# K and Q of later tiles projected with tokens stationary and laid out by transposing DMAs

## The chip, the cores and the metric

The kernel runs on one core of a Trainium2 chip. A core has a matrix engine (TensorE, PE, with its weight loads shown as PEld), VectorE (DVE), ScalarE (ACT), GpSimd (POOL), and SyncE (SP), which here only issues DMAs. Each engine works through its own queue in order and waits for others by semaphores; sixteen DMA engines move the data. The metric is the device time of one execution in microseconds, given as the median of several runs.

## The reference

A block of a transformer with two halves, on 2048 tokens of width 448, in bf16. Six modulation vectors come from a conditioning row. The first half is attention with 16 heads of width 28, in which each query sees itself and the 255 tokens before it. The second is a gated MLP whose gate is mixed over the tokens by a full 2048 x 2048 matrix.

```python
mod = (_silu(c) @ w_mod).reshape(c.shape[0], 6, 1, -1)
sa, ca, ga, sb, cb, gb = ...
h = _layernorm(x, axis=-1) * (1 + ca) + sa
x = x + ga * _A_ref(h, A_wqkv, A_wo)
h = _layernorm(x, axis=-1) * (1 + cb) + sb
x = x + gb * _B_ref(h, B_w_in, B_w_sp, B_b_sp, B_w_out)
# _A_ref: q, k, v = x @ wqkv; softmax over the window of 256; (p @ v) @ wo
# _B_ref
z = _gelu(jnp.einsum('bsd,df->bsf', x, w_in))
z1 = z[..., :Fh].copy()
z2 = _layernorm(z[..., Fh:], axis=-1)
g = jnp.einsum('ts,bsf->btf', w_sp, z2) + b_sp[None, :, None]
return jnp.einsum('bsf,fd->bsd', z1 * g, w_out)
```

## The kernel before

The tokens are 16 tiles of 128, in four blocks of four tiles. The work has three stages. In the first, attention, each tile is normalized (statistics on DVE, the reciprocal root on POOL), turned so that the width lies on the partitions (block 0 by PE, blocks 1 to 3 by transposing DMAs from `xn` into `hT`), modulated in place, and projected to Q, K and V. Scores, exponentials, masks, the product with V, the output projection and the second normalization follow per tile. In the second stage PE computes the two halves of the MLP's input (`z2` at L1120, `z1T` at L1141). In the third it multiplies with the spatial matrix (L1166) and the output matrix (L1185). The spatial matrix comes from memory through 32 transposing DMAs of 128 x 1024: 16 into `wspA`, which the first half of the third stage needs whole, and 16 into `wspB`.

Heads are 28 wide, and the scores are computed with 32 rows per head, four heads beside each other on PE's rows. So Q and K must stand as 4 groups of 4 heads x 32 rows (28 used), tokens along the free axis. `WQK` holds the weights padded to 32 columns per head. For K, one tile at a time: 4 groups x 4 chunks of the width, 16 matmuls with 128 weights columns stationary and 128 tokens streamed (L821), copied to `KT` by ACT or DVE (L833, L834). For Q of blocks 1 to 3, a whole block at a time: 4 groups x 4 chunks of 512 tokens (L763), copied to `qT` (L772, L773). Some of the queries' far halves are also needed in a block-diagonal form, `QBD`, in which each head's queries stand on that head's rows only: four copies of 32 rows per block make it (L790, L791), and one pair of matmuls per tile uses it (L967). V is projected with the tokens stationary and 448 columns of unpadded weights streamed (L841).

The order of all work is fixed ahead. Each operation has a number; the string `PLAN` lists them, a letter for the engine (p, a, d, t, s for PE, ACT, DVE, POOL and SP), the number, and the buffers it takes. Each engine runs its part of the list in order, and semaphore waits are derived from the data and the buffers. The list is the result of a search, with durations and waits of a model. `turn` is the helper that issues a transposing DMA on SP: turned are the normalized rows (`xn`, `xn2`), the attention output (`o_sb`) and the spatial matrix. SP runs these and the plain loads and stores in one queue.

Of the kernel before, what the change touches and what calls it, by code (L numbers as in the profile page):

```python
# [5 lines left out]
BF16 = mybir.dt.bfloat16  # L6
# [6 lines left out]
a0 t30 d24 s1 d27 d26 d25 d23 d22 p51.1 t31 p60.3 s2 t32 p52.2 t35 p59.0 s4 p61.1 p55.0 s6 a3 p58.0 p63.0 a5  # L13
s10 t36 p40.1 a7 s8 p69.2 a9 p75.3 d114 s12 p65.1 p53.0 t33 d112 p68.2 s11 t34 p54.3 d115 p77.0 d113 p50.3 s13
a41 p71.0 t116 a43 p46.0 s15 d117.0 t29 p74.2 d118.3 p62.0 p64.2 p47 a42 a44 p57.0 p48.1 d106 d86 p76.0 p49
a107 t104 p129.6 p67.3 d87 d105 p126.4 t37 a130 p82.3 p56.3 t111 p84.1 d127 p81.1 p73.1 a131 p83.3 p66.0 d128
t38 p72.0 p141.1 d110 d121 p78.0 a108 t109 p70.2 p150.3 d119 p142 d122 d120 p79.2 d184 p151 t123 a143 p138.0
a152 t28 d125.2 p139 d124.3 p85.0 p147.6 d178 a140 p132.2 d185 p148 d182 a133 p144.7 d179 d180 p135.1 a134
p153.0 d183 a136 d181 p371.0 d246 t186 a137 p145 d248 p154 a372.4 t39 p165.1 d187.3 t190 d242 s194 p166 t188
a149 t192 d45 p377.0 a146 d373 p156.6 d167 a378.6 t189.1 p157 d244 p159.7 t191.2 a158 p395.0 d193.0 a155 s196  # L20
d379 p172.6 a396.5 d249 d247 p173 d243 p175.1 a174 s197 p160 d88 t89 d245 a397 p176 d168 p94.0 t250 p95 d177
s195 a171 p402.0 a161 d96 t254 p97.1 t256 a403.1 p98 d398 s14 d375 p162.7 d400 p374.0 p163 a404 d381 p90.0 d99
p376 d201 a199 p422.0 d198 d251.0 p380 p382 d200 p91 s258 a423.0.0 p211.1 d93 d92 d407 d170 d252 p212 p218.0
d255.1 t253.2 a164 d383 s260 p429.0 d169 a213 t257.3 p219 a430.3 p399.1 p205.1 s16 d220 p206 d384.2 p202.0
d306 s385 p203 a207 d426 p401 p447.0 a204 p208.1 s804 a448.4.1 d310 p209 d405 p227.0 d431 p228 s259 t102
p424.1 p406 p408 a425 p454.0 d229 a210 d409 p427.0 d312 a455.1 p230.0 t101 d410.1 p221.1 p231 d216 d214 d451
s411 t103 p428 p222 a232 p80.3 p472.0 d456 s261 a223 p432 a215 p224.0 a473.5.2 p225 s21 p233.1 p433 s807
p449.0 d434 t100 d226 a217 p479.0 d435.0 a450 t262 p234 d308 s436 a480.0 p474.0 p236.0 t263 d311 d313 d235
p452.0 p237 d476 s806 p453 a475 p496.0 a238 d307 d481 t265 d264 p412.1 a497.3.0 p457 p386.0 p387 p458 d309
d459 d388 d460.1 t314 t320 p413 p498.0 p521.0 a499 a522.1.1 p272.0 d414 p523.0 p273 p269.1 s461 p270 p477.0  # L30
d415 d274 d321.2 d316 s20 p503.0 a271 d500 t317.3 p275.0 p478 s323 p276 p266.1 p267 p482 a504.4 a524 p546.0
p483 t318 d389 d277 d319.1 a268 d505 d484 p282.0 d390 d278 p283 a547.5.2 p437.1 p548.0 p438 s18 d485.1 d525
p501.0 p528.0 d439 d440 d315.0 s486 s325 a284 a529.0 a549 a279 p502 p288.0 p291.1 p292 p289 d290 p553.0 d530
d293 p506 p507 p239.0 s322 p240 a554.3 a241 p526.1 t391 p527 s324 p531 a280 d550 p571.0 p532 p462.0 d508 d281
d416 d509.2 d392.1 d533 d441 t442 t417 a572.4.0 p463 p294.1 d534.1 d464 p573.1 p295 p578.0 a296 p300.0 s510
p285.1 p286 a579.0 p551.1 p301 p552 p595.0 d555 t329 t418 d327 d287 d302 d575 p511.1 p512 p556 d513 t328 a326
a596.1.1 a574 p336.0 p337 p557 p602.0 s535 p576.0 a338 p577 d558 d559.0 a603.3 p536.0 d393 p339.1 p537 p340
d580 p620.0 d538 d599 a341 p581 p297.0 p597.0 s17 s394 p487.1 d465 p298 a621.6.2 d539 a598 a299 p488 p582
p645.0 d583 p600.1 s808 d584.1 p622.1 p333.0 d489 p330.1 d624 d604 d466 p331 p334 a646.4.0 s585 d490 a332
p627.0 p601 t467 t443 t468 d335 d491 p346.1 d345 t444.1 p605 p347 p586.0 p587 a628.0 a348 p652.0 p358.1 d514  # L40
d649 a623 s560 a653.1 d588 p359 p606 p349.0 p350 p625.0 d629 a360 a351 p670.0 d589 d654 d607 p352.1 p303.0
p304 s19 a671.2.1 p353 p626 a344 a305 d608.2 t469.2 p630 p677.0 d354 d419.0 p631 p647.0 p364.1 a678.6 p561.0
p562 p365 d342 a648 p694.0 d420 t445 d674 d632 d343 d540 t470 s446 d633.0 p650.1 s803 a366 p672.1 d679 d563
a695.5.2 s609 d564 p367.1 p651 s421 t492 p655 p368 p656 p701.0 t541 a673 t542 d543.1 d657 p355.0 p675.0 a369
a702.3 t544 d658.2 p676 d493.0 p680 p356 d698 d565 d357 p696.0 p681 t566 d515 d682 p719.0 a697 d494 d590
# [1223 lines left out]
```

## Time and profile before

| what | value |
|---|---|
| time, three runs | 275.18 to 275.75 us, median 275.42 us |
| the profiled execution | span 273.2 us from the first to the last instruction |
| busy in the span | PE 267.1, PEld 155.3, DVE 160.4, ACT 126.4, POOL 111.4 us |
| attention, 20 to 107.6 us | PE 86.0, ACT 81.1, DVE 80.8 us busy |
| MLP input, 107.6 to 152.7 us | PE 45.0, DVE 37.3, ACT 27.9 us busy |
| spatial and output matrix, 152.7 to 270.6 us | PE 117.4 us busy |
| granted TensorE clock | 1.00 throughout |

The profile shows one execution. Its span leaves out what lies around the instructions, which the runs' times take in. PE's busy time is not its peak, because matmuls are pipelined; a length in the chain of waits (start, length, what) is the nearest to what an instruction costs in a row of others. The chain follows the work that ended last backwards, from each step to what released it. A group's row gives line, engine, operation, output and inputs, shapes and count, then the busy time, the mean of one in ns, and the idle time before it with what ended it.

### The profile page before, as it was taken

The numbers are of one execution on the slowest core, as the hardware profiler recorded it, in microseconds if no ns is written. First come the engines' busy times: TensorE is split into PE (matmuls) and PEld (weight loads), VectorE is DVE, ScalarE is ACT, GpSimd is POOL, SyncE is SP. The second block draws the span as 40 slices with busy tenths as digits, with TensorE's granted clock in tenths as the row PEclk, the third lists the DMA queues.
The fourth block names the chain that finished last, engine by engine and source line by source line (L and its number), as shares of the span: only waits on it lengthen the run. The fifth ranks groups of instructions, "written<-read, shape, count | busy, mean of one in ns | idle before, by whom it ended". The sixth has DMA issues, their size and how long they took to land.

```text
span 273.2 us, 8371 instructions
## 1 busy us (share of the span) xinstructions
PE 267.1 (98%) x3741; PEld 155.3 (57%) x3751; DVE 160.4 (59%) x344; ACT 126.4 (46%) x149; POOL 111.4 (41%) x147
## 2 busy tenths in 40 slices
PE   8999999999999999999999999999999999999996
PEld 6976676777667866554554444444444444444453
DVE  3798999989889999949889210221222022152244
ACT  5799999899989988567666400000000000000000
POOL 6455298305033286547448003354543023061330
PEclk9999999999999999999999999999999999999999
DMA  7999846453234573957789996000000000001003
GB/s 209 299 244 132 127 103 122 122 101 109 64 103 67 91 73 72 185 117 134 117 176 175 217 186 118 0 0 0 2 0 0 0 2 0 34 17 36 34 34 118
DMA packets 67301, 25.54 MB, mean 93 GB/s; under 512 B 58497, under 2 KB 66178, under 8 KB 67266
## 3 DMA queue, kind: packets, MB, share of 16 engines
q1 hardware_dynamic: 66016, 24.02, 44.5%
q10 hardware_dynamic: 1250, 0.99, 1.3%
q8 instruction: 29, 0.48, 0.7%
q14 instruction: 6, 0.05, 0.1%
HBM read 9.01 MB, written 1.84 MB: 40 GB/s over the span
## 4 chain that ended last, share of the span: by engine, by line
PE 80%; ACT 8%; DMA 6%; DVE 3%; SPq 2%; issue 1%
PE ps L1166 35%; PE ps L1120 8%; PE ps L1141 8%; PE ps L1185 8%; ACT PW L912 6%; DMA wmodB<-in_w_mod_dram 6%; PE ps L1000 5%; PE ps L956 4%; PE ps L1026 4%; PE ps L763 3%; PE ps L821 2%; PE ps L841 2%; DVE PT L973 1%; ACT QBD L790 1%; PE ps L967 1%
## 5 line engine op out<-in xcount | busy, mean ns | idle before, releaser
L1173 POOL TENSOR_TENSOR z1T<-tmpg,z1T 128x512 bf16<-128x512 bf16 x28 | 32.0, 1152 | 77.3 <-DVE tmpg L1170 77.3
L912 ACT ACTIVATE PW<-ps 128x2048 bf16<-128x2048 f32 (+1 forms) x42 | 59.9, 1452 | 5.4 <-PE ps L956 3.9
L1170 DVE TENSOR_TENSOR tmpg<-ps,bsp_bc 128x512 bf16<-128x512 f32 x28 | 18.9, 689 | 73.8 <-PE ps L1166 62.6
L1166 PE MATMUL ps<-wspB,z 128*128 128x512 bf16 x219 | 49.7, 379 | 0.3
L1166 PE MATMUL ps<-wspA,z 128*128 128x512 bf16 x219 | 49.1, 379 | 0.4 <-issue 0.2
L633 POOL TENSOR_TENSOR rs_all<-mv_all,neghalf 128x1 f32<-128x1 f32 (+2 forms) x37 | 22.5, 635 | 45.6 <-DVE mv_all L631 45.6
L1166 PEld LDWEIGHTS ps<-wspA,z 128*128 128x128 bf16 x224 | 21.8, 98 | 26.6 <-issue 0.4
L1166 PEld LDWEIGHTS ps<-wspB,z 128*128 128x128 bf16 x224 | 21.9, 98 | 26.2
L973 DVE TENSOR_TENSOR PT<-PW,mask 128x2048 bf16<-128x2048 bf16 x28 | 34.0, 1219 | 0.0
L1000 PE MATMUL ps<-Vaug,PT 128*128 128x32 bf16 x496 | 25.8, 177 | 0.0
L1000 PEld LDWEIGHTS ps<-Vaug,PT 128*128 128x128 bf16 x496 | 22.9, 96 | 3.3 <-issue 0.4
L1120 PE MATMUL ps<-w_in,hT 64*128 64x448 bf16 x224 | 22.0, 349 | 0.0
L1185 PE MATMUL ps<-w_out_g,z1T 128*128 128x448 bf16 (+2 forms) x119 | 22.0, 341 | 0.0
L1141 PE MATMUL ps<-hT,w_in 64*128 64x512 bf16 x196 | 22.0, 376 | 0.0
L1000 PE MATMUL ps<-Vaug,PW 128*128 128x32 bf16 x224 | 21.2, 176 | 0.0
L629 DVE BATCH_NORM_STATS2 st_all<-z 128x6 f32<-128x448 bf16 x32 | 18.4, 608 | 4.4 <-ACT z L1127 4.3
L629 DVE BATCH_NORM_STATS2 st_all<-x_sb 128x6 f32<-128x448 bf16 x32 | 19.2, 614 | 2.7 <-DMA x_sb<-in_A_x_dram 2.5
L1195 DVE TENSOR_TENSOR fin<-ps,x_sb 128x448 bf16<-128x448 f32 (+1 forms) x16 | 9.5, 612 | 16.7 <-PE ps L1185 11.6
L1000 PEld LDWEIGHTS ps<-Vaug,PW 128*128 128x128 bf16 x224 | 17.9, 96 | 1.9
L821 PE MATMUL ps<-hT,WQK 112*128 112x128 bf16 x256 | 18.7, 219 | 0.0
L1149 ACT ACTIVATE z1T<-ps 128x512 bf16<-128x512 f32 x28 | 14.5, 603 | 8.8 <-PE ps L1141 8.7
L956 PE MATMUL ps<-qT,KT 32*128 32x128 bf16 (+5 forms) x1344 | 17.1, 197 | 0.9 <-ACT PW L912 0.6
(108 smaller groups left out, 355.0 us busy)
## 6 DMA issues: line engine op xcount, KB each, us to landing
wmodB<-in_w_mod_dram SPq DMA_DIRECT2D x1, 1568.0 KB, 15.3
out_dram<-fin SPq DMA_DIRECT2D x14, 112.0 KB, 1.7
x_sb<-in_A_x_dram SPq DMA_DIRECT2D x3, 448.0 KB, 7.9
w_in<-in_B_w_in_dram SPq DMA_DIRECT2D x3, 448.0 KB, 4.2
w_out_g<-in_B_w_out_dram SPq DMA_DIRECT2D x1, 784.0 KB, 6.4
bsp_bc<-in_B_b_sp_dram SPq DMA_DIRECT2D x1, 512.0 KB, 5.3
x_sb<-in_A_x_dram SPq DMA_DIRECT2D x2, 224.0 KB, 4.9
hT<-xn SPq DMA_TRANSPOSE x28, 2.9
```

The costliest lines, as they stand in the source:

```text
L629: st = [dve(0.62, lambda e, t=t, o=12 - 6 * (n - ci), s=s: e.bn_stats(st_all[:, slot, t, o:o + 6], s()), deps(t), prio) for ci, s in enume ...
L633: return pool(0.4 + 0.15 * len(tiles), lambda e: e.tensor_tensor(rs_all[:, slot, a:b], mv_all[:, slot, a:b, 1], neghalf[:, 0:b - a], ALU.pow),
L821: km = lambda g, kc, start, stop, h=h, t=t: lambda e: e.matmul(ps[:, h.slot[0], g * 128:(g + 1) * 128], lhsT=WQK[0:CP, kc, 16 + 4 * g:20 + ...
L912: ex = act(xdur, lambda e, out_ap=out_ap, in_ap=in_ap: e.activation(out_ap(), in_ap(), ACT.Exp, scale=SCALE), [s] + list(after), v - 8.0 + ...
L956: fm.append(lambda e, hm=hm, qi=qi, key=key, kn=kn, lo=lo, hi=hi, col=col, p0=p0, t=t, j=j: e.matmul(ps[p0:p0 + kn, hm.slot[t], col:col + ...
L973: mk2 = lock_d(1.2, lambda e, hp=hp, at_w=at_w, pad=pad, at_f=at_f, cols=cols, j=j: e.tensor_tensor(cols(hp.slot[0] * 2048, [[256, 8], [12 ...
L1000: fns.append(lambda e, hp=hp, hO=hO, hi=hi, bi=bi, kb=kb, hd=hd, nb=nb, a=at[hi][bi], p_of=p_of: e.matmul(ps[:, hO.slot[0], 32 * hd:32 * h ...
L1120: return lambda e, kc, p0, start, stop: e.matmul(ps[:, hs[t % 2].slot[hf], 0:D], lhsT=hT[p0:p0 + 64, kc, t * 128:(t + 1) * 128], rhs=w_in[ ...
L1141: return lambda e, kc, p0, start, stop: e.matmul(ps[:, hs[b // 2].slot[b % 2], :], lhsT=w_in[p0:p0 + 64, kc, ft * 128:(ft + 1) * 128], rhs ...
L1166: m = pe(16 * MMS, [lambda e, h=h, si=si, ft=ft, tb=tb: e.matmul(ps[:, h.slot[0], :], lhsT=z2[:, si, ft * 128:(ft + 1) * 128], rhs=(wspA i ...
L1173: u = pool(1.16, lambda e, ht=ht, ft=ft, tb=tb: e.tensor_tensor(z1T[tb][:, ft, :], tmpg[:, ht.slot[0], :], z1T[tb][:, ft, :], ALU.mult), [ ...
L1185: return [lambda e, ft=ft: e.matmul(ps[:, h.slot[0], 0:hi - lo], lhsT=z1T[t // 4][:, ft, (t % 4) * 128:(t % 4 + 1) * 128], rhs=w_out_g[:, ...
```

## The change

For tiles 4 to 15 Q and K are projected like V: the 128 tokens of a tile are stationary, and 448 columns of unpadded weights are streamed, four matmuls for K and four for Q (L805 in the changed kernel). ACT or DVE copies the result, tokens on the partitions, into a staging tile with the heads 32 columns apart: one copy for K into one of two `kst` (L817, L818), two copies for Q into one of two `qst` (L835, L836; even and odd groups apart). A transposing DMA on SP then lays each out: `kst`, 512 columns, into a ring of 8 tiles that is now `KT`, and `qst`, 1280 columns, into a ring of 4 tiles, `qring`. Of its ten blocks of 128 columns two are plain groups and eight hold one head each of the other groups with zeros around it, so that the block-diagonal form comes out of the same transfer. The zeros are set once (POOL, L531 and L532). The copies into `QBD` remain for block 0 alone, and tiles 0 to 3 are projected as before. `qring` and the staging tiles lie in the first half of `wspA`, so those eight loads wait until all scores and all turns of Q and K are done. The waits that paced the projections are gone. The list of the order was searched anew, so the order on all engines differs.

```diff
+    KR, QR, QB_N = 8, 4, 10
+    KT, kt_off, _ = alloc("KT", [128, 4, KR * 128], BF16)
+    wq_st, _, _ = alloc("wq_st", [128, DC, 2 * D], BF16)
+    kst = [alloc("kst0", [128, H, 32], BF16)[0]]
...
-    QBD, _, qbd_bytes = alloc("QBD", [128, 2, 4, 2, 256], BF16, at=wspA_off)
-    qT, _, qt_bytes = alloc("qT", [128, 2, 4, 512], BF16, at=wspA_off + qbd_bytes)
+    qring, _, qr_bytes = alloc("qring", [128, QR, QB_N, 128], BF16, at=wspA_off)
+    qst, _, qs_bytes = alloc("qst", [128, 2, QB_N * 128], BF16, at=wspA_off + qr_bytes)
+    kst.append(alloc("kst1", [128, H, 32], BF16, at=wspA_off + qr_bytes + qs_bytes)[0])
...
+    t_qsz = [pool(0.8, lambda e, i=i: e.memset(qst[:, i, :].bitcast(F32), 0.0), prio=-60.0) for i in range(2)]
+    t_ksz = [pool(0.2, lambda e, i=i: e.memset(kst[i][:, :, DH:32], 0.0), prio=-60.0) for i in range(2)]
...
-            mms = [lambda e, h=h, g=g, kc=kc, tb=tb: e.matmul(
-                ps[:, h.slot[0], :], lhsT=WQK[0:CP, kc, 4 * g:4 * g + 4, :].rearrange("p a b -> p (a b)"),
-                rhs=hT[0:CP, kc, tb * 512:(tb + 1) * 512], start=(kc == 0), stop=(kc == DC - 1)) for kc in range(DC)]
-            m = pe2(4 * MMS, mms, [evs, t_wqk], v + 1 + k * 0.1, [h])
...
+                def by_tokens(part, h, t=t, evs=evs, v=v):
+                    return pe2(4 * MMD, [lambda e, kc=kc: e.matmul(
+                        ps[:, h.slot[0], 0:D], lhsT=hT[0:CP, kc, t * 128:(t + 1) * 128], rhs=wq_st[0:CP, kc, part * D:(part + 1) * D],
+                        start=(kc == 0), stop=(kc == DC - 1)) for kc in range(DC)], [evs, (t_wk, t_wq)[1 - part]], v + 1, [h])
...
+                K_ready[t] = turn("d_k%d" % t, lambda t=t: KT[:, :, t % KR * 128:(t % KR + 1) * 128], lambda hs=hs: kst[hs.slot[0]][:].rearrange("p h e -> p (h e)"), [ev], v + 1)
+                hs.until.append(K_ready[t])
...
+                Q_ready[t] = turn("d_q%d" % t, lambda t=t: qring[:, t % QR], lambda hs=hs: qst[:, hs.slot[0], :], [q_evs], v + 1, lat=1.6)
+                hs.until.append(Q_ready[t])
...
-        deps = [t_mB, t_gg] if si > 7 else [S_of[8], S_of[9], S_of[10], S_of[11], S_of[WSP][0], q_dma[2]] if si in (0, 1, 4, 5) else [all_S, list(q_dma.values())]
+        deps = [t_mB, t_gg] if si > 7 else [all_S, [Q_ready[t] for t in range(4, NT)], [K_ready[t] for t in range(4, NT)]]
```

Three places of the order. SP late in attention, about tiles 10 to 15; before, it holds the turns of the attention output (`o_sb`) and of the second normalization (`xn_91`, the tile `xn2`) and a few loads:

```order
L432 DMA w_in<-in_B_w_in_dram 128x1792
L465 DMA_TRANSPOSE hT<-xn_91 128x4x128
L465 DMA_TRANSPOSE wspA<-in_B_w_sp_dram 128x1024
L465 DMA_TRANSPOSE hT<-o_sb 128x4x128
L465 DMA_TRANSPOSE hT<-xn_91 128x4x128
L465 DMA_TRANSPOSE hT<-o_sb 128x4x128
```

The same stretch of the changed kernel, where `xn_95` is `xn2` and `kst_76` and `kst_87` are the two staging tiles:

```order
L471 DMA_TRANSPOSE KT<-kst_76 128x4x128
L471 DMA_TRANSPOSE KT<-kst_87 128x4x128
L471 DMA_TRANSPOSE hT<-o_sb 128x4x128
L471 DMA_TRANSPOSE hT<-xn_95 128x4x128
L471 DMA_TRANSPOSE hT<-o_sb 128x4x128
L471 DMA_TRANSPOSE KT<-kst_76 128x4x128
L471 DMA_TRANSPOSE qring<-qst 128x10x128
```

The turns of K and Q stand between those that were there, and the early loads of `wspA` have left.

SP after attention, from the load of the output matrix on; before:

```order
L861 DMA w_out_g<-in_B_w_out_dram 128x7x448
L465 DMA_TRANSPOSE wspA<-in_B_w_sp_dram 128x1024 x2
L465 DMA_TRANSPOSE hT<-o_sb 128x4x128
L465 DMA_TRANSPOSE hT<-xn_91 128x4x128 x4
L465 DMA_TRANSPOSE wspB<-in_B_w_sp_dram 128x1024
L465 DMA_TRANSPOSE wspA<-in_B_w_sp_dram 128x1024 x2
L465 DMA_TRANSPOSE hT<-xn_91 128x4x128 x3
L465 DMA_TRANSPOSE wspA<-in_B_w_sp_dram 128x1024
L465 DMA_TRANSPOSE hT<-xn_91 128x4x128
L465 DMA_TRANSPOSE wspA<-in_B_w_sp_dram 128x1024 x5
L465 DMA_TRANSPOSE wspB<-in_B_w_sp_dram 128x1024
L465 DMA_TRANSPOSE wspA<-in_B_w_sp_dram 128x1024
```

In the changed kernel, from the turn of tile 15's normalized rows (the last of the two `xn_95` here) to the last load of `wspA`:

```order
L471 DMA_TRANSPOSE wspB<-in_B_w_sp_dram 128x1024
L471 DMA_TRANSPOSE hT<-xn_95 128x4x128 x2
L471 DMA_TRANSPOSE wspB<-in_B_w_sp_dram 128x1024 x2
L471 DMA_TRANSPOSE wspA<-in_B_w_sp_dram 128x1024 x3
L471 DMA_TRANSPOSE wspB<-in_B_w_sp_dram 128x1024
L471 DMA_TRANSPOSE wspA<-in_B_w_sp_dram 128x1024 x3
L471 DMA_TRANSPOSE wspB<-in_B_w_sp_dram 128x1024
L471 DMA_TRANSPOSE wspA<-in_B_w_sp_dram 128x1024
```

Between the last turn of `xn2` and the last load of `wspA` stood 6 large loads of `wspA` and one of `wspB`; now 7 and 4. Counted from the load of the output matrix there were 11 of `wspA`, 2 of `wspB` and 9 turns, and now there are 14, 6 and 9, behind a first load of `wspB` that waits for the last probabilities.

DVE around a copy of K late in attention; before, that of tile 14, from PSUM to `KT`:

```order
L1014 RECIPROCAL rec_all<-ps 128x16
L1016 TENSOR_TENSOR o_sb<-ps,rec_all 128x4x112
L834 CAST KT<-ps 128x4x128
L651 TENSOR_SCALAR xn_91<-x_sb,rs_all,nm_all 128x448
L791 COPY QBD<-qT 32x512
```

In the changed kernel that of tile 13, from PSUM to the staging tile:

```order
L1026 TENSOR_TENSOR o_sb<-ps,rec_all 128x4x112
L983 TENSOR_TENSOR PT<-PW,mask_60 128x2048
L637 BN_STATS st_all<-x_sb 128x6
L639 BN_AGGR mv_all<-st_all 128x2
L818 CAST kst_76<-ps 128x16x28
L983 TENSOR_TENSOR PT<-PW,mask_60 128x2048 x2
```

A mask multiply and a statistics pair now stand directly ahead of the copy, and the copies into `QBD` have left this stretch.

306 lines of the change are left out of this document (142 added, 164 removed).

## The prediction

> **What bounds the kernel now.** I read the page first (span, busy shares, shares of the chain), then the busy time of each engine in five stretches, then the chain of waits in order of time, then the groups by form, and last the timeline of SP, because the change puts 24 transfers on SP's queue.
>
> ```profile
> span 273.2 us, 8371 instructions
> PE 267.1 (98%) x3741; PEld 155.3 (57%) x3751; DVE 160.4 (59%) x344; ACT 126.4 (46%) x149; POOL 111.4 (41%) x147
> PE 80%; ACT 8%; DMA 6%; DVE 3%; SPq 2%; issue 1%
> ```
>
> ```profile
> 0.00:10.00 10.00, 8.89 (x80) 7.32 (x81) 4.30 (x18) 6.57 (x9) 6.07 (x17) 1.00 0.86 231
> 20.00:60.00 40.00, 39.31 (x1069) 28.11 (x1067) 35.81 (x73) 37.48 (x40) 19.36 (x18) 1.00 0.67 120
> 60.00:107.60 47.60, 46.66 (x1427) 34.83 (x1427) 44.99 (x84) 43.65 (x42) 20.35 (x29) 1.00 0.42 80
> 107.60:152.70 45.10, 44.97 (x452) 21.60 (x454) 37.32 (x98) 27.88 (x42) 24.84 (x42) 1.00 0.85 155
> 152.70:270.60 117.90, 117.37 (x557) 55.13 (x565) 28.02 (x44) 2.31 (x5) 34.95 (x31) 1.00 0.18 38
> ```
>
> The columns of the second are the stretch, its length, then PE, PEld, DVE, ACT and POOL busy, the granted clock (1.00), the share of the DMA engines and GB/s. The span is 273.2 us against a median of 275.42 us; I keep these 2.2 us around it unchanged and sum against the span. From 107.6 us on PE alone sets the time. Before it, from 20 to 107.6 us (attention), PE is busy 86.0 of 87.6 us, but ACT 81.1 and DVE 80.8 too: three engines are nearly full, and one that gets lighter helps only as far as the other two let it.
>
> ```profile
> 46.21 0.22 PE ps L967 x2
> 47.73 1.30 PE ps L763 x6
> 52.29 0.54 PE ps L956 x32
> 53.23 0.90 PE ps L821 x16
> 65.25 0.76 PE ps L841 x4
> 107.59 1.62 PE ps L1120 x16
> 110.38 0.29 PE ps L1000 x12
> 152.57 0.16 issue
> 152.73 10.74 PE ps L1166 x49
> 270.61 0.33 DVE o_sb L1195
> ```
>
> These pieces of the chain (start, length, what) are PE's prices where it does not wait: a 512-wide matmul 1.30/6 = 0.217 us, a 128-wide one 0.90/16 = 0.056, a 448-wide one 0.76/4 = 0.190, a half tile's scores 0.54, the pair of L967 0.22, twelve of L1000 0.29. The last probabilities are used up at 110.38 + 0.29 = 110.67 us, and the first matmul with the spatial weights (L1166) starts 42.1 us later, at 152.73, with no wait named before it but 0.16 us of issue.
>
> **The change part by part.** PE first. Removed: per tile of tiles 4 to 15 sixteen 128-wide K matmuls, 192 x 0.056 = 10.8 us, and 48 Q matmuls of 512, 48 x 0.217 = 10.4 us. Added: 96 of 448 columns, 96 x 0.190 = 18.2 us. PE gets 3.0 us less, all of it before the last probabilities. The rest of PE's instructions is the same in kind and number.
>
> ```profile
> L833 ACT ACTIVATE KT<-ps 128x512 bf16<-128x512 f32 x11 | 6.6, 604 | 0.4 <-PE ps L821 0.4
> L845 ACT ACTIVATE Vaug<-ps 128x448 bf16<-128x448 f32 x10 | 5.5, 552 | 0.1
> L846 DVE CAST Vaug<-ps 128x448 bf16<-128x448 f32 x6 | 3.6, 604 | 0.2 <-PE ps L841 0.2
> L834 DVE CAST KT<-ps 128x512 bf16<-128x512 f32 x5 | 3.4, 679 | 1.9 <-PE ps L821 1.7
> L791 DVE COPY QBD<-qT 32x512 bf16<-32x512 bf16 x7 | 3.3, 472 | 0.2
> L790 ACT ACTIVATE QBD<-qT 32x512 bf16<-32x512 bf16 x5 | 3.1, 628 | 0.1
> L815 ACT ACTIVATE QBD<-qT 32x256 bf16<-32x256 bf16 x1 | 0.4, 412 | 0.0
> L1195 DVE TENSOR_TENSOR o_sb<-ps,x_sb 128x160 bf16<-128x160 f32 x1 | 0.3, 325 | 0.0
> PEld ps L956 <- ACT PW L912: 3.9, 10, 0.7
> ```
>
> Copies out of PSUM. The K copy shrinks from 512 to 448 columns (0.604 to 0.552 us on ACT, 0.679 to 0.604 on DVE): 12 copies, about -0.7 us. Twelve Q copies of 512 (about 12 x 0.62 = 7.5 us) become 24 of 224 columns; no row has that form, the nearest are 0.325 (160 columns, DVE) and 0.412 (256, ACT), I take 0.38: 9.1 us, +1.6. The twelve 512-wide copies into QBD go: 3.3 + 3.1 = 6.4 us. So the two engines lose 5.5 us, most of it on ACT, which keeps 3.9 us of PE's waits (the last row: weight loads of the scores waiting for the exponentials, ten times). I count this relief at nothing in the sum, since DVE is as full and its share in it is small (its projection copies go from about 14 to 13.5 us); between nothing and -1.0 us is the bound.
>
> ```profile
> L499 POOL MEMSET Vaug<- 128x768 bf16 x1 | 1.2, 1214 | 0.0
> ```
>
> POOL fills two qst buffers and two strips of kst, at this row's rate 0.6 to 1.0 us each for the large ones. They lie in the first 10 us, where POOL is busy 6.07 us; this costs nothing, and up to 1 us if the first normalization waits for them.
>
> Now the handover. A projection used to go PE, copy, PE; now it goes PE, copy, SP, transposing DMA, PE.
>
> ```profile
> L465 SPq DMA_TRANSPOSE hT<-xn x28: 1188/1265/2212, 16.6 to 132.7; - x28
> hT<-xn SPq DMA_TRANSPOSE x28, 2.9
> wspA<-in_B_w_sp_dram SPq DMA_TRANSPOSE x16, 3.9
> ...
> 55.55 4.92 SPq L465 DMA_TRANSPOSE hT<-xn  x3
> 109.61 5.50 SPq L465 DMA_TRANSPOSE wspA<-in_B_w_sp_dram  x2
> 132.65 1.25 SPq L465 DMA_TRANSPOSE hT<-xn  x1
> 143.20 1.29 SPq L465 DMA_TRANSPOSE wspA<-in_B_w_sp_dram  x1
> 149.38 16.93 SPq L465 DMA_TRANSPOSE wspB<-in_B_w_sp_dram  x11
> 149.40:166.30 16.90, 16.69 (x92) 7.54 (x91) 3.88 (x9) 3.67 (x8) 2.35 (x3) 1.00 1.07 195
> ```
>
> The first row is min/median/max of SP's time for one issue in ns, the next two the median us from issue to landing, then five pieces of SP's timeline, and the DMA engines while eleven large transposes run alone. One issue costs SP about 1.25 us whatever its size; a 128x512 one lands after 2.9 us. Alone, the 128x1024 ones follow each other every 16.93/11 = 1.54 us with the DMA engines full (1.07). So K (half of it) takes 0.77 us of DMA time and Q (1280 columns) 1.9; no row has Q, its landing lies between 2.9 and 3.9 us plus what a quarter more columns add.
>
> How long the new path may take I read from the order of the change, as PE work between the last projection matmul and the scores that need it. Mostly it is 6 to 18 us. The two shortest are K of tile 8 (fourteen 448-wide, 24 of L1000, one half tile's scores, one pair: 4.0 us) and K of tile 13 (twelve, 48, one, two pairs: 12 x 0.190 + 48 x 0.024 + 0.54 + 2 x 0.22 = 4.4 us). The path itself is at least 0.604 + 2.9 = 3.5 us. Ahead of K 13's copy on DVE stand a mask multiply, a statistics instruction and its aggregation.
>
> ```profile
> L973 DVE TENSOR_TENSOR PT<-PW,mask 128x2048 bf16<-128x2048 bf16 x28 | 34.0, 1219 | 0.0
> L629 DVE BATCH_NORM_STATS2 st_all<-x_sb 128x6 f32<-128x448 bf16 x32 | 19.2, 614 | 2.7 <-DMA x_sb<-in_A_x_dram 2.5
> ```
>
> That is 1.22 + 0.61 + about 0.2 = 2.0 us more, 5.5 in all: PE would stand about 1.0 us before tile 13's scores, and the scores of both its halves, the exponentials and the masks queue behind. K 8 has only 0.6 us of work ahead of it and comes just in time. I take +1.0 us for the handover, with bounds of -1.0 (ACT's relief) and the rival below.
>
> Last, the spatial weights. qring and the staging tiles lie where wspA's first half lands, so its loads can't start early: by the two orders, 5 of 16 stood on SP ahead of the last probabilities, now 2, and the new order puts 6 loads of wspB ahead of the last of wspA instead of 2. Before, 18 issues went out from 109.61 to 132.65 us, 1.28 us each, then the turn of tile 15's normalized rows, then seven large ones at 1.54: the last wspA was issued at 143.20 and landed some 3.9 us later, 5.6 us ahead of its use. After the change the same count runs from the last probabilities, on which the first wspB waits: 0.3 us, 17 issues x 1.28 = 21.8, tile 15's turn 1.3, eleven large ones x 1.54 = 16.9, and 2.6 from the end of the issue to landing: 42.9 us, against the 42.1 us that PE needs. L1166 then waits 0.8 us. If the mixed part does not overlap (9 x 1.54 + 8 x 1.3 = 24.3) it is 3.3 us; if the DMA engines run ahead, nothing. The rest of wspB, ten issues later, is due 17 us of PE work after that and takes 16: no wait.
>
> Sum: -3.0 (PE) + 1.0 (handover) + 0.8 (wspA) = -1.2 us: span 272.0, time 275.42 - 1.2 = 274.2 us.
>
> **The rivals.** First, slower: SP's in-order queue becomes the pace of attention. From K 4's turn to Q 15's the order has 45 transposes and 5 plain loads on SP (0.6 us each): 45 x 1.25 + 3 = 59 us, against 64 us of PE work in between: 93% full, with waits in order inside. It decides when the gain is gone, at 45 m + 3 = 64 + 3.0, a mean issue of m = 1.42 us. For it: three in a row took 4.92 us, 1.64 each, and the longest 2.2. Against it: the median is 1.265, and the DMA engines, at 0.67 and 0.42 before, get 12 x 2.7 = 32 us of work in 87.6 less three wspA loads, about 0.85. At 1.5 us it costs 6.4 us: 275.42 - 3.0 + 6.4 + 0.8 = 279.6 us.
>
> The Trainium skill, "TensorE: Matmul & The Clock Gate", section "Why this matters for your kernels", warns that a PE gap of more than about 3 us brings the half clock back. This trace has no such gap (clock 1.00 in every stretch), so no run here shows it; under this rival one late transpose could add it, by an estimate from that page up to some 2 us, which is not in the numbers.
>
> Second, slower: wspA is later than I count, at 3.3 us, with the handover's 1.0: 275.42 - 3.0 + 1.0 + 3.3 = 276.7 us. For it: the DMA share of 0.85 in 107.6 to 152.7 before, with three large loads more to come. Against it: the 1.28 per issue fits the part before.
>
> Third, faster: everything is hidden, 275.42 - 3.0 = 272.4, and 271.4 with ACT's relief. For it: most handovers have 6 us and more; large transposes that issue every 1.29 us, as the one at 143.20 did, instead of 1.54 would land wspA 2.8 us earlier, ahead of its use. The Trainium skill, "Advanced Engine Details and Errata", section "X-Bar Transpose (TRN2)", speaks for this one: it has transposing DMAs as fast as plain ones, 350 to 400 GB/s. By it a 256 KB load would take about 0.7 us (an estimate from that page) and the issue would bound. The row above has 195 GB/s with full engines, so I give it little.
>
> **How the numbers follow.** Forecast as summed 0.40 (own range 273.0 to 275.0), SP's queue 0.33, wspA late 0.13, all hidden 0.14. A difference under 0.2% (0.55 us) can't be told from none here. Faster: 0.36 of the forecast's case and all 0.14 of the third, 0.50. Within: 0.04 + 0.05 + 0.03 = 0.12. Slower: 0.28 + 0.10 = 0.38. The range goes from 271.6, inside the third, to 279.4, just under the queue's price: what is left out is the longest queue and the full relief, 2 in 10.
>
> **What the profile after would show.** Right: the 448-wide projection at about 0.19 us apiece in the chain; the last L1000 of attention some 2 us earlier than 110.67; ahead of tile 13's scores a wait for K's transpose; L1166's first matmul waiting a little for wspA; issue medians of 1.25 to 1.3 us. Wrong: scores waiting for qring or KT in many tiles and SP without idle time from 40 to 100 us (the queue); several us before L1166 (wspA); or a chain in attention that is DVE's throughout, so that PE's 3.0 us come back as its waiting.

## The result and the profile after

The changed kernel took 299.24 us in the median of five runs (298.28 to 303.98), the kernel before, run beside it, 275.75 us: a ratio of 1.084, 95% interval 1.078 to 1.089. It is slower by some 23 us, where 274.2 us was forecast and 279.4 was the upper end of the range. The profiled execution of the changed kernel is the longest of its five (303.98 us), so its stages are together up to 5 us longer than those of a usual run; the experiments below give the usual lengths. In all that follows a median takes in every execution, while a ratio and its interval leave out those that ran over 1.5% longer than the fastest of the same kernel.

Busy time by stage, the kernel before: from the start to the first score (15.09 us), to the end of the last product with V (110.67), to the first matmul with the spatial weights (152.73), to the end. Columns: stretch, its length, busy time of PE, PEld, DVE, ACT, POOL, granted clock, share of the DMA engines, GB/s.

```profile
0.00:15.09 15.09, 13.98 (x157) 11.84 (x158) 9.12 (x34) 10.20 (x16) 7.79 (x20) 1.00 0.95 257
15.09:110.67 95.58, 93.88 (x2624) 68.48 (x2625) 88.65 (x174) 87.14 (x89) 43.79 (x54) 1.00 0.57 106
110.67:152.73 42.06, 41.90 (x409) 19.85 (x410) 34.28 (x94) 26.77 (x41) 24.84 (x42) 1.00 0.87 159
152.73:273.20 120.47, 117.37 (x557) 55.13 (x565) 28.34 (x45) 2.28 (x5) 34.95 (x31) 1.00 0.18 40
```

The same four stages of the changed kernel:

```profile
0.00:20.74 20.74, 14.98 (x146) 11.87 (x147) 10.91 (x37) 7.44 (x14) 11.29 (x27) 0.92 0.96 236
20.74:133.21 112.47, 97.98 (x2492) 63.35 (x2492) 88.85 (x169) 84.25 (x89) 40.52 (x54) 0.94 0.82 126
133.21:181.55 48.34, 42.54 (x407) 19.41 (x405) 37.54 (x101) 31.12 (x46) 18.61 (x32) 1.00 0.89 162
181.55:302.25 120.70, 118.07 (x569) 55.24 (x567) 28.59 (x45) 1.95 (x4) 36.76 (x33) 1.00 0.16 35
```

Three stages are longer: the start by 5.6 us, attention by 16.9, the MLP's input by 6.3; the last is unchanged. In attention PE stands 14.5 us, against 1.7 before, its clock is at half speed for part of the time (0.94 in the mean), and the DMA share rose from 0.57 to 0.82. The span's shares of the chain, by engine, on the page of the changed kernel (before: PE 80%, DMA 6%):

```profile
PE 60%; DMA 17%; DVE 8%; ACT 8%; SPq 3%; POOL 1%; issue 1%; DVEq 0%; ACTq 0%; POOLq 0%
```

Pieces of that chain in order of time (start, length, what), changed kernel:

```profile
5.33 10.03 DMA wq_st<-in_A_wqkv_dram
37.07 5.46 DMA qring<-qst
48.10 4.34 DMA KT<-kst
95.60 0.77 PE ps L805 x4
105.60 3.91 DMA KT<-kst
```

PE's new matmul costs what was forecast (0.77 / 4 = 0.19 us). The rest are transfers. A part of the weights of K and Q lands at 15.4 us, on the chain to the first score, and the list of waits below adds 3.2 us for `wmodA`: late loads make the start's loss. In attention the transposes themselves lie on the chain. SP's issues in the changed kernel (min/median/max ns of one, first and last start):

```profile
L471 SPq DMA_TRANSPOSE KT<-kst x12: 1188/1268/1956, 35.3 to 113.4; - x12
L471 SPq DMA_TRANSPOSE qring<-qst x12: 1339/1734/2732, 37.1 to 114.7; - x12
L471 SPq DMA_TRANSPOSE hT<-xn x28: 1188/1265/2612, 20.1 to 157.7; - x28
L471 SPq DMA_TRANSPOSE hT<-o_sb x16: 1190/1274/2742, 43.9 to 141.9; - x16
```

And a piece of SP's timeline, changed kernel:

```profile
105.60 2.96 SPq L471 DMA_TRANSPOSE KT<-kst  x2
108.61 1.27 SPq L471 DMA_TRANSPOSE hT<-o_sb  x1
109.92 2.15 SPq L471 DMA_TRANSPOSE hT<-xn  x1
112.11 1.27 SPq L471 DMA_TRANSPOSE hT<-o_sb  x1
```

Each issue begins where the last one ends. From K 4's turn at 35.3 us to Q 15's at 117.5, SP issues 50 transfers in 82.2 us and is busy for 77.4 of these. PE's waits (engine, tile, line, what it waited for: us in total, times, longest), changed kernel:

```profile
PE ps L966 <- DMA KT<-kst: 5.3, 3, 2.4
PE ps L554 <- DMA wmodA<-in_w_mod_dram: 3.2, 1, 3.2
PE ps L977 <- DMA qring<-qst: 3.1, 1, 3.1
PE ps L1119 <- DVE hT L1060: 2.7, 1, 2.7
PE ps L1119 <- ACT z L1126: 2.6, 1, 2.6
```

By this list the scores' waits for K and Q (8.4 us) are the largest part. The experiments show that these waits are not the cause.

### The profile page after: what moved, and what is told of

Read it like the earlier page. It is cut to its first block, busy times and chain, and to the rows that moved or that the text cites. A ratio compares the mean times of both kernels' runs of the same rounds, so it can differ in the third digit from the quotient of the medians.

```text
span 302.3 us, 8140 instructions
## 1 busy us (share of the span) xinstructions
PE 273.6 (91%) x3607; PEld 149.9 (50%) x3607; DVE 165.9 (55%) x350; ACT 124.8 (41%) x151; POOL 107.2 (35%) x144
## 4 chain that ended last, share of the span: by engine, by line
PE 60%; DMA 17%; DVE 8%; ACT 8%; SPq 3%; POOL 1%; issue 1%; DVEq 0%; ACTq 0%; POOLq 0%
PE ps L1165 32%; PE ps L1184 7%; DMA qring<-qst 6%; ACT PW L922 5%; PE ps L966 4%; PE ps L1140 4%; DMA wq_st<-in_A_wqkv_dram 3%; PE ps L805 3%; PE ps L1119 3%; DMA hT<-xn 3%; DMA KT<-kst 3%; DVE st_all L637 2%; PE ps L1010 2%; PE ps L843 2%; DMA x_sb<-in_A_x_dram 2%; SPq L471 2%
## 5 line engine op out<-in xcount | busy, mean ns | idle before, releaser
L1165 PE MATMUL ps<-wspB,z 128*128 128x512 bf16 x224 | 50.0, 379 | 0.0
L1165 PE MATMUL ps<-wspA,z 128*128 128x512 bf16 x224 | 49.3, 379 | 0.0
L641 POOL TENSOR_TENSOR rs_all<-mv_all,neghalf 128x1 f32<-128x1 f32 (+2 forms) x37 | 23.7, 661 | 37.0 <-DVE mv_all L639 37.0
L983 DVE TENSOR_TENSOR PT<-PW,mask 128x2048 bf16<-128x2048 bf16 x28 | 35.3, 1270 | 1.1 <-ACT PW L922 1.1
L1165 PEld LDWEIGHTS ps<-wspA,z 128*128 128x128 bf16 x224 | 21.8, 98 | 26.7 <-DVE z L1131 0.5
L1165 PEld LDWEIGHTS ps<-wspB,z 128*128 128x128 bf16 x224 | 21.9, 98 | 26.2
L1119 PE MATMUL ps<-w_in,hT 64*128 64x448 bf16 x224 | 23.2, 349 | 5.5 <-DVE hT L1060 2.7
L805 PE MATMUL ps<-wq_st,hT 112*128 112x448 bf16 x96 | 24.8, 380 | 0.8 <-ACT qst L835 0.7
L1010 PE MATMUL ps<-Vaug,PT 128*128 128x32 bf16 x496 | 24.6, 178 | 0.9 <-ACT PW L922 0.4
L1010 PEld LDWEIGHTS ps<-Vaug,PT 128*128 128x128 bf16 x496 | 22.1, 97 | 5.2 <-issue 1.3
L1140 PE MATMUL ps<-hT,w_in 64*128 64x512 bf16 x196 | 22.8, 376 | 0.6 <-ACT z1T L1148 0.6
L966 PE MATMUL ps<-qring,KT 32*128 32x128 bf16 (+5 forms) x1152 | 15.3, 201 | 6.5 <-DMA KT<-kst 5.3
L843 PE MATMUL ps<-wv,hT 112*128 112x448 bf16 x64 | 18.3, 386 | 1.9 <-DVE qst L836 1.8
L966 PEld LDWEIGHTS ps<-qring,KT 32*32 32x32 bf16 (+1 forms) x1152 | 12.0, 92 | 14.3 <-ACT PW L922 7.3
```

The lines of the kernel that those rows point to most:

```text
L805: return pe2(4 * MMD, [lambda e, kc=kc: e.matmul(ps[:, h.slot[0], 0:D], lhsT=hT[0:CP, kc, t * 128:(t + 1) * 128], rhs=wq_st[0:CP, kc, part ...
L843: m = pe2(4 * MMD, [lambda e, h=h, t=t, kc=kc: e.matmul(ps[:, h.slot[0], 0:D], lhsT=hT[0:CP, kc, t * 128:(t + 1) * 128], rhs=wv[0:CP, kc, ...
L966: fm.append(lambda e, hm=hm, qi=qi, key=key, kn=kn, lo=lo, hi=hi, col=col, p0=p0, t=t, j=j: e.matmul(ps[p0:p0 + kn, hm.slot[t], col:col + ...
L983: mk2 = lock_d(1.2, lambda e, hp=hp, at_w=at_w, pad=pad, at_f=at_f, cols=cols, j=j: e.tensor_tensor(cols(hp.slot[0] * 2048, [[256, 8], [12 ...
L1010: fns.append(lambda e, hp=hp, hO=hO, hi=hi, bi=bi, kb=kb, hd=hd, nb=nb, a=at[hi][bi], p_of=p_of: e.matmul(ps[:, hO.slot[0], 32 * hd:32 * h ...
L1119: return lambda e, kc, p0, start, stop: e.matmul(ps[:, hs[t % 2].slot[hf], 0:D], lhsT=hT[p0:p0 + 64, kc, t * 128:(t + 1) * 128], rhs=w_in[ ...
```

## The experiments

Each was timed in four executions beside seven of the kernel before. "More than before" is counted from the median of the kernel before in the same comparison.

**The order of the first loads, put back.** SP's first loads and ACT's, as before:

```diff
-SP:  s1 s2 s10 s4 s8 s12 s11 s6 s13 s15      ACT: a0 a5 a7 a41 a3 a43 a9
+SP:  s1 s2 s4 s6 s10 s8 s12 s11 s13 s15      ACT: a0 a3 a5 a7 a9 a41 a43
```

(6 and 7 are the two parts of K's weights, 2 to 5 those of `wmodA`.)

> The changed kernel, with the first loads issued in the order that they had before (on SP and on ACT); all else as changed. Theory A (the new order of the first loads makes everything 5.6 us late, since wq_st lands at 15.4 us and half of wmodA late, and nothing behind gives it back): 299.2 - 5.6 = 293.6 us, between 292.5 and 295, first score at about 15 us instead of 20.7. Rival B (the 16 DMA engines are full in the first 15 us and the order only decides which tensor is late, or the lead is used up later by SP's queue): 298.5 to 299.5 us.

296.19 us, ratio 1.073 (1.065 to 1.080): 3.1 us less than the changed kernel by the two ratios. The first score comes at 16.1 us. Stages after the start, this run:

```profile
16.11:123.06 106.95, 95.17 (x2491) 62.57 (x2490) 89.76 (x169) 83.95 (x89) 42.20 (x53) 0.97 0.89 134
123.06:172.51 49.45, 42.70 (x407) 19.67 (x409) 37.55 (x101) 31.35 (x46) 18.94 (x32) 1.00 0.89 167
```

The median lies 1.2 us above theory A's range and well below rival B's: of the 4.6 us that the start gives back in the two profiles, some 3 us reach the end (a rough size, since the intervals of the two ratios overlap a little). What is left is 11.4 us in attention (106.95 against 95.58) and 7.4 us behind it.

**The same order in the kernel before.** The reverse edit.

> The kernel before, with the changed kernel's order of the first loads on SP and ACT and nothing else. Theory A (the order itself costs the time): 275.4 + 5.6 = 281.0 us, between 279.5 and 282.5. Rival B (the late start belongs to the other work at the start, such as the memsets and the other order on PE, or is made up later): 275.2 to 276.5 us.

280.81 us, ratio 1.016 (1.011 to 1.020): 4.5 us more. The first score moves to 20.48 us and attention takes 95.57 us, as before. PE's longest wait is new:

```profile
PE ps L546 <- DMA wmodA<-in_w_mod_dram: 3.9, 1, 3.9
```

So theory A holds from both sides in kind: the order alone costs 3 to 4.5 us.

**A third staging buffer for Q.**

```diff
-    qsR = Res(range(2), [(i,) for i in range(2)])
+    qsR = Res(range(3), [(i,) for i in range(3)])
```

> The changed kernel with a third staging buffer for Q (qst three deep instead of two), given out in turn; one more memset on POOL. Theory C (a copy into qst that waits for a transfer to free the buffer stands at the head of DVE's or ACT's queue and holds back the exponentials and masks behind it; 5.9 us and 3 x about 1.3 us of such waits stand in the trace): 299.2 - 3 to -7 us, 292 to 296. Rival D (SP issues the transposes one behind the other without a pause from 35 to 117 us, so a copy that starts earlier only waits longer for SP): 298 to 300.5 us.

299.04 us, ratio 1.081 (1.073 to 1.088). No change, as rival D has it: waits for one of Q's two staging buffers are not the cause (theory C).

**Scores that wait for no handover.**

```diff
-                need = [Q_ready[j]] + [K_ready[kb] for kb in kbs]
+                need = [Q_ready[j]] + [K_ready[kb] for kb in kbs] if j < 4 else [K_ready[i] for i in range(4)]
```

> The changed kernel with the scores of tiles 4 to 15 reading K of tiles 0 to 3 for both operands, so that they wait for no transposed K or Q; projections, copies, staging buffers and all transposing transfers stay, and the output is not the reference's. Theory E (the 17 us lost between the first score and the last P.V product are waits of the scores for the landing of K and Q): 299.2 - 15 to -18 us, about 282, with the 5.6 us of the start and some 1 us left. Theory C (staging buffers block DVE and ACT ahead of the exponentials): about half stays, 289 to 293 us. Rival D (SP's full queue makes the other transposes, h and o, late, whoever reads K and Q): 294 to 299 us.

298.62 us, ratio 1.083 (1.078 to 1.088): nothing gained. The 8.4 us of waits for K and Q are gone and others have taken their place; attention takes 106.4 us, as in the run with the old loads (106.95). Theory E, the obvious reading of the waits, is refuted: without these waits the stage is no shorter. That is what rival D had said.

**The transposes as a load alone.** All 24 are issued, from a buffer that doesn't change; nobody waits for them and they wait for no copy.

```diff
-... lambda hs=hs: qst[:, hs.slot[0], :], [q_evs], v + 1, lat=1.6)
-                hs.until.append(Q_ready[t])
+... lambda: still[:], [t_qsz], v + 1, lat=1.6)
+                hs.until += q_evs
```

> The changed kernel with all 24 transposes of K and Q still issued by SP at their places and with their sizes, but from a buffer that never changes: no copy waits for them, they wait for no copy, and the scores of tiles 4 to 15 read K of tiles 0 to 3 (the output is not the reference's). What stays is their load on SP and on the DMA engines. Counted from the first score to the end of the last P.V product, which took 95.6 us before and 106.4 us in the run without handover: theory C (copies that wait for a staging buffer stop DVE and ACT, and PE behind them, and the clock halves behind such a gap): about 97 us there, so 288 to 291 in all. Theory D (the load alone, a full queue on SP that makes h and o late): 104 to 107 there, 296 to 299 in all.

298.23 us, ratio 1.078 (1.069 to 1.086); attention takes 105.7 us. With no staging wait and no handover wait left, nearly all of the loss is still there: theory D, the load alone.

**The same load in the kernel before.**

```diff
+            extra[(t, n)] = turn("d_extra%d_%d" % (t, n), lambda n=n, at=at, to=to: to[:, at:at + n]...,
+                                 lambda n=n: still[:, 0:n], [t_mB, t_gg, t_still, extra.get((t - 2, n))], 0.0)
```

> The kernel before, with 24 transposes added on SP between its own, of the sizes of K's and Q's (12 of 128x512, 12 of 128x1280), from a buffer of zeros into buffers that nobody reads then; nobody waits for them. Theory D (the load alone delays the transposes of h and o that the tiles wait for): 8 to 11 us more, 284 to 287. Theory C (the load is carried, the staging is what costs): 0 to 2.5 us more, 275.5 to 278.5.

295.79 us, ratio 1.073 (1.068 to 1.077): 20.2 us more, twice what theory D said, so the load alone is enough, and costs more than was understood. All of it stands in attention. That stage in this run:

```profile
15.70:131.17 115.47, 100.42 (x2624) 70.71 (x2625) 89.19 (x174) 87.27 (x89) 39.08 (x54) 0.94 0.93 137
```

And PE's longest waits in this run:

```profile
PE ps L1027 <- DVE Vaug L847: 3.7, 1, 3.7
PE ps L1001 <- DVE o_sb L1017: 3.5, 1, 3.5
PE ps L1027 <- DMA hT<-o_sb: 3.2, 2, 2.6
```

None of these waits names an added transfer. They are waits for the attention output's turn and for DVE, which itself stands for SP's older transposes (at the longest 4.9 us for `hT<-xn` and 4.2 for `hT<-o_sb`). PE is also slower: it is busy 100.42 us with the same matmuls that took 93.88, at a mean clock of 0.94. That is 6.5 of the 19.9 us by which the stage grew. From 33 us to the last product with V, SP was busy 63% of the time before (49.2 of 77.7 us, 39 issues) and 96% here (94.0 of 98.2 us, 64 issues; the 24 added ones took 39.1 us).

**The end's order on SP.** In the changed kernel, w_sp's transposes set back behind those of `o_sb` and `xn2` as far as before.

```diff
-s843 s826 s671 s822 s696 s835 s785 s646 s621 s821 s825 s824 s720 s827 s770 s836 s745 s795
+s843 s826 s785 s671 s696 s646 s621 s822 s835 s821 s825 s720 s770 s745 s824 s795 s827 s836
```

(785 turns `o_sb` of tile 15; 621, 646, 671, 696, 720, 745, 770, 795 turn `xn2` of tiles 8 to 15; the others load w_sp.)

> The changed kernel with one edit in SP's order behind the last probabilities: the transposes of w_sp stand behind those of o of tile 15 and of h of tiles 8 to 15 as far as they did before (ten stand ahead of the last one of h now, six did before). Theory G (from the end of the last P.V product to the first spatial product it takes 49.5 us against 42.1 because h of the last tiles is queued on SP behind w_sp): 3 to 5.5 us less, 293.5 to 296. Rival H (ACT, busy 31.3 us there against 26.8, and the order on PE and DVE hold the end back whatever SP does): at most 1 us less, 298 to 299.5.

299.74 us, ratio 1.085 (1.078 to 1.091): no gain, as rival H had it. The chain of this run shows one thing that holds the end back:

```profile
164.68 0.92 ACT z L1126
...
165.62 1.28 ACT L527
...
166.91 0.20 ACT ex_sb L527
...
167.12 1.28 ACT L1126
```

The 1.28 us pieces are ACT's table loads. The small exponential of L527, which fetches the table for exp ahead of its use, stood eighth on ACT before. In the new order it stands among the evictions of z, after the last real exponential: the table for exp comes in and the one for z has to come back. PE waits 2.6 us for that z.

**No transposes of K and Q at all.**

```diff
-                K_ready[t] = turn("d_k%d" % t, ...)
+                K_ready[t] = pool(0.1, lambda e, t=t: e.memset(still[:, t:t + 1], 0.0))
```

> The changed kernel without the 24 transposes of K and Q of tiles 4 to 15 (a memset of one column on POOL stands in each place); projections and copies stay, the scores of tiles 4 to 15 read K of tiles 0 to 3, and the output is not the reference's. If load and staging together make the loss between the first score and the last P.V product, that stage takes 93 to 96 us and the whole 286 to 289 (start and end stay as late as in the changed kernel). If the copies on ACT and DVE or the new order on the engines make it (theory F: 5.5 us of copies more), it takes over 100 us and the whole 292 or more.

286.68 us, ratio 1.038 (1.032 to 1.044), 12.6 us less than the changed kernel by the ratios. Attention in this run:

```profile
18.97:116.44 97.47, 91.96 (x2492) 61.59 (x2492) 89.11 (x169) 83.65 (x89) 40.51 (x78) 1.00 0.49 86
```

The granted clock is 1.00 there again. 97.47 us is 1.5 us above the range given for load and staging, and below the 100 us of theory F: the copies on ACT and DVE, all still there, are at most a small part. The MLP's input still takes 47.2 us against 42.1 before, so that loss has another cause than the 24 transposes.

**The table load put back.**

```diff
-... a1010 a952 a42 a958 a1011 ...      (42: the exponential of L527)
+... a41 a3 a43 a42 a9 ...
```

> The changed kernel with one ACT instruction at its place of before: the small exponential that fetches ACT's table for exp stands among the first instructions again and not between the evictions of z after the last probabilities, where the trace shows two table loads of 1.28 us, one on each side of it, and PE idle for 2.56 us right behind. Theory J (these 2.6 us stand on the path to the end): 2.0 to 2.8 us less, 296.4 to 297.2. Rival K (PE would wait at that place or a little later for something else, h of tile 15 or DVE): less than 0.8 us less, 298.4 to 299.4.

296.72 us, ratio 1.076 (1.071 to 1.081): 2.2 us less by the ratios, 2.5 by the medians, in theory J's range, though the intervals of the two ratios overlap. The MLP's input took 48.6 us in this run's profile, against 49.5 to 50.3 in the four runs above that change neither this nor SP's order at the end and keep the transposes.

**Issue or bytes?** In the kernel before, the 24 added transposes made small, then only the 12 large ones.

```diff
-        for at, n in ((1280, 512), (0, 1280)):
+        for at, n in ((1280, 128), (0, 256)):
```

> The kernel before with the same 24 added transposes at the same places as in the run in which they cost 20.2 us, but small: 12 of 128x128 and 12 of 128x256, 21% of the bytes. Theory L (what costs is the issue: SP gives out one transpose in about 1.3 us, however small, and stands for each): 13 to 20 us more than before, 288.5 to 296. Theory M (what costs is the moved data: the 16 DMA engines and the transposing itself): 1 to 5 us more, 276.5 to 280.5.

291.59 us, ratio 1.058 (1.053 to 1.063): 15.9 us more than before, with 21% of the bytes. SP's rows of this run (`wspA` and `fin` are where the idle transfers land) and its attention:

```profile
L466 SPq DMA_TRANSPOSE wspA<-still x12: 1127/1246/2496, 36.8 to 107.5; - x12
L466 SPq DMA_TRANSPOSE fin<-still x12: 1217/1241/2152, 44.1 to 113.3; - x12
16.11:128.83 112.72, 98.22 (x2624) 70.32 (x2625) 89.18 (x174) 87.34 (x89) 37.58 (x54) 0.95 0.62 100
```

```diff
-        for at, n in ((1280, 512), (0, 1280)):
+        for at, n in ((0, 1280),):
```

> The kernel before with only the 12 large ones (128x1280) of the 24 added transposes: half of the issues and 71% of the bytes. Theory L (issues): SP was busy 63% of the time from 33 us to the last P.V product, 12 issues of 1.4 us bring that to about 85%, so 2 to 9 us more, 277.5 to 284.5. Theory M (bytes): 12 to 16 us more, 287.5 to 291.5.

281.40 us, ratio 1.022 (1.014 to 1.030): 5.7 us more, with 71% of the bytes. The same rows of this run:

```profile
L466 SPq DMA_TRANSPOSE wspA<-still x6: 1336/1811/2465, 35.9 to 96.9; - x6
L466 SPq DMA_TRANSPOSE fin<-still x6: 1419/2276/2457, 40.6 to 101.9; - x6
15.90:117.17 101.27, 95.95 (x2624) 69.06 (x2625) 89.26 (x174) 87.31 (x89) 40.03 (x54) 0.98 0.90 140
```

Many small ones cost nearly three times what few large ones cost, and they cost it while the DMA engines are little busier than before (a share of 0.62 in attention, 0.57 before; 0.90 with the large ones). So it is not the bytes and not full DMA engines: theory L, SP's time to issue. In SP's time the three runs fall into line. The added issues took 39.1, 33.8 and 23.4 us of it (all, small, large only), and the kernel took 20.2, 15.9 and 5.7 us more: about one for one above some 18 us (an estimate from these three), of the 28.5 us that SP had free in the kernel before (77.7 - 49.2). So a part of a queue's idle time is not free: loss begins before the queue is full.

**The three orders together.** First loads, table, and an order at the end on SP that goes further than the one above (o of tile 15 ahead of any w_sp, the first half of w_sp ahead of the second).

> The changed kernel with three of its orders put right and the 24 transposes kept: the first loads as before, the exponential that fetches the table among the first instructions, and behind the last probabilities the transposes of o of tile 15 and of h of tiles 8 to 15 ahead of most of w_sp on SP, the first half of w_sp ahead of the second. If the three losses are separate (3.1 us by the run with the first loads as before, 2.6 us for the table, 1 to 3 us for h of tile 15): 290.5 to 293 us. If the full queue takes back what the ends give: 294 to 297 us. By either it stays above the kernel before.

295.19 us, ratio 1.068 (1.061 to 1.074): not the 290.5 to 293 of three separate losses, but in the range for a gain that is taken back. The MLP's input takes 43.2 us, nearly as before, where it took 48.6 with the table mended alone and 49.5 with the first loads alone: SP's order counts too, taken far enough. h of tile 15 landed 25.0 us behind the last product with V here, 28.8 us with the milder edit, 24.6 us in the kernel before. But the last stage takes 123.8 us against 120.5, since the edit made the second half of w_sp late; PE's longest wait in this run:

```profile
PE ps L1165 <- DMA wspB<-in_B_w_sp_dram: 3.1, 1, 3.1
```

**The same, with the second half of w_sp earlier.** One transpose of each half of w_sp moves ahead of o of tile 15 (785).

```diff
-s547 s785 s397 s826 ...
+s547 s826 s843 s785 s397 ...
```

> The changed kernel with the three orders put right as in the run before (first loads, table, and h of tiles 8 to 15 ahead of most of w_sp), and one transpose of each half of w_sp moved into the 5.3 us in which SP waited for o of tile 15, so that the last of the second half lands 2.6 us earlier. If the wait of 3.1 us for the second half was made by the edit: 3 us less than the 295.2 us, 291 to 293 us. If SP's queue takes it back at another place: 294 to 296 us.

292.08 us, ratio 1.050 (1.039 to 1.061, from two executions): in the range given if the wait came from the edit. The traces don't bear that reason out. PE's wait for `wspB` is still there: 4.1 us in this run's profile, which is of its longest execution (298.70 us), and 2.5 and 2.0 us in the profiles of the two runs below, which keep this order. What brought the 3 us stays open.

**The three orders and no transposes of K and Q.** The kernel just shown, with the memsets of POOL in the place of the 24 transposes.

> The kernel of the run beside it (three orders put right) without the 24 transposes of K and Q: a memset of one column on POOL stands in each place, and the scores of tiles 4 to 15 read K of tiles 0 to 3, so the output is not the reference's. If the transposes on SP's queue and the three orders are all of the loss: 276 to 280 us, within 1.5% of the kernel before. If a part of the loss has another cause (the copies on ACT and DVE, the order on PE): 282 us or more.

Its profiled execution took 279.66 us at clock 1.00, three others 283.9 to 285.5 at 0.98 to 0.99; the median is 284.30, and no ratio is on record. The stages of the profiled one:

```profile
0.00:16.30 16.30, 14.73 (x144) 11.92 (x144) 10.33 (x37) 9.07 (x16) 11.37 (x27) 1.00 0.94 261
16.30:111.80 95.50, 91.88 (x2492) 61.55 (x2492) 88.18 (x170) 82.34 (x88) 42.47 (x78) 1.00 0.51 94
111.80:154.30 42.50, 42.20 (x407) 19.59 (x404) 36.52 (x101) 28.22 (x43) 18.81 (x32) 1.00 0.83 158
154.30:277.70 123.40, 118.25 (x569) 55.20 (x567) 28.57 (x45) 1.97 (x5) 36.77 (x33) 1.00 0.21 45
```

Start, attention and MLP's input are within 1.2, 0.1 and 0.4 us of the kernel before. The remaining 2.9 us are in the last stage, where my order of w_sp still lets PE wait 2.5 us. So in this execution the 24 issues and the three orders account for the loss in the first three stages. As a whole it is just inside the 276 to 280 us that I gave for that; the median lies in the range given for another cause. Where the other three lost 4 to 6 us more, no trace of them tells, so this account rests on one execution.

**Six plain loads off SP.** The kernel with the three orders and all transposes; the load of wo and the five of w_in go out from ACT.

```diff
-    t_wo = load2("d_wo", "sp", ...
+    t_wo = load2("d_wo", "act", ...
```

> The kernel with the three orders put right, with all 24 transposes, and the six plain loads of wo and w_in issued by ACT at the same places of the program instead of SP. Theory L (SP's issue time is the pace): six issues of 0.58 us are 3.5 us off a queue that is busy 90% of the time, so 2 to 4.5 us less than the run with the three orders, 287.5 to 291 us. Rival N (only transposes hold each other up, the plain loads slip in between): within 1 us of that run.

290.37 us, ratio 1.054 (1.046 to 1.062), against 292.08 and 1.050 for the kernel without this edit: not told apart. Attention took 104.3 us in its profile against 107.1 in that of the first run with the three orders, which is in theory L's direction. I leave it open. No version tried beats the kernel before.

## Why the prediction was wrong

Point by point, by its own steps.

- **PE, -3.0 us: right in price, worth nothing.** The new matmul costs 0.19 us. Without the transposes and with the three orders mended PE is busy 91.88 us in attention against 93.88, which is 2.0 less and not 3.0 (the other 1.0 was not followed up). Even there the lighter PE bought nothing: attention took 95.50 against 95.58 us.
- **Copies, counted at 0: right.** The 224-wide copies took 0.36 us on ACT and 0.39 on DVE (0.38 taken); ACT is 2.9 us lighter in attention, DVE not at all.
- **Memsets, 0:** nothing in the runs speaks against it.
- **Handover, +1.0 us: the wrong kind of term.** K of tile 13 did land late, as the step said, and PE waited 2.4 us for it instead of 1.0. But its copy ended at 103.3 us and SP, busy with two other transposes, issued its turn only at 105.6. Taking every handover wait away gained 0.6 us by the medians, which is within the noise: a wait for one transfer was only the place where the late queue showed.
- **wspA late, +0.8 us: wrong.** The first spatial matmul (L1165 now) waited for no `wspA` in the changed kernel. It was late by 6 to 7 us, counted from the last product with V, for two other reasons: SP's order at the end, which delays `o_sb` and `xn2` of the last tiles (with the table mended alone the stage takes 48.6 us, with SP's further order too 43.2), and the table load (2.2 to 2.5 us of the whole). SP's order was never tried far enough by itself, so the split between the two is rough.
- **SP's queue put at nothing: the step that failed.** "One issue costs SP about 1.25 us whatever its size" and "Against it: the median is 1.265" kept the queue out of the sum and gave it a chance of 0.33. Two things in that step were wrong. A median stood where a mean was needed. The rival was to decide at a mean of 1.42; in the kernel before, the 33 transposes from 33 us to the last product with V take 45.7 us of SP, 1.38 each, and 45 x 1.38 + 3 = 65.1 us already fill the 64 us. In the run with the first loads put back the 45 transposes take 69.7 us, 1.55 each, since some three in ten are held for over 1.5 us. And the formula lets SP fill up before anything is lost, while 23.4 us of added issues, less than the 28.5 us that SP had free, cost 5.7 us. With the measured issues the formula gives 69.7 + 3 - 64 - 3.0 = 5.7 us for attention; 11.4 were measured in that run (106.95 - 95.58). 3.3 of them are PE at half clock; the rest is not taken apart. "Three in a row took 4.92 us", 1.64 each, is near what came, but three issues make no mean, and that they fit is luck. The prediction's own sign for this case, SP without idle time, came true (77.4 of 82.2 us). The rival had the mechanism for attention and priced it too low (6.4 us at a mean of 1.5, so 279.6 us in all).
- **What was never read: the rest of the order.** The prediction followed the new order at three places and took the others as unchanged. The first loads (3 to 4.5 us) and one ACT instruction (2.2 to 2.5 us) moved too. Both stood in the order, and neither was in the sum, in a rival or in the range. The last turns of `o_sb` and `xn2` did stand in one of the three places, but there the prediction counted the loads of w_sp alone.
- **The half clock.** The prediction cited the Trainium skill, "TensorE: Matmul & The Clock Gate", section "Why this matters for your kernels", left it out of the numbers, and allowed 2 us. It came true: in all five executions of the changed kernel the granted clock is 0.97 to 0.98 in the mean against 1.00. With the first loads put back PE is busy 95.17 us in attention, without the transposes 91.88: 3.3 us of slower matmuls.

## What to carry to other kernels

A queue that issues in order has a budget like an engine. Add up the time of the new issues at the mean of one, not the median, over the stretch in which they go out, set it against the queue's idle time there, and don't count all of that as free: here 23.4 us of issues in 28.5 us of idle time cost 5.7 us, and 39.1 us cost 20.2. A wait named in the profile is a place and not yet a cause; take it away, and if the time stays, look at what feeds everything that waits. Where an order was searched anew, compare all of it, the first loads and one-off instructions too: here the search moved them, and it cost 5 us and more.

## What the runs showed of the hardware

SP took 1.24 to 1.25 us in the median to issue a transposing DMA in the rows that hold those of 128x128 and 128x256, 1.27 for one of 128x512 in the changed kernel's rows, and, run by run, 1.4 to 2.3 for one of 128x1280 (1.34 at the least): some 1.2 us per issue however small the transfer, and more only for the largest.

In these traces the half clock comes in pieces of 3.4 us or twice that, and the length of PE's gap alone doesn't decide. Four stretches of the run with the end's order on SP changed, columns as above:

```profile
50.10:51.80 1.70, 0.00 (x0) 0.00 (x0) 0.00 (x0) 1.57 (x2) 0.97 (x3) 0.99 0.10 5
51.80:55.20 3.40, 3.32 (x56) 1.69 (x57) 3.28 (x6) 0.27 (x1) 0.00 (x0) 0.51 0.77 154
159.40:162.30 2.90, 0.01 (x2) 0.00 (x0) 2.12 (x5) 0.98 (x3) 2.06 (x3) 1.00 0.90 197
162.30:165.70 3.40, 3.32 (x36) 1.68 (x38) 3.37 (x10) 1.00 (x2) 2.22 (x4) 1.00 0.91 178
```

A gap of 1.7 us was followed by 3.4 us at half clock, one of 2.9 us was not. In the run with the first loads put back a gap of 1.8 us at 62.1 us was followed by 3.4 us at half clock, one of 2.6 us at 159.5 was not. The Trainium skill, "TensorE: Matmul & The Clock Gate", section "Why this matters for your kernels", speaks of gaps over about 3 us. Here shorter ones were enough, though not each time. What else decides it no run here tells apart.
